# Cosine attention and an MLP mixer in one kernel: norms pair by pair, another order of squares, loads and sums, two more pairs transposed on TensorE

## The chip, the cores and the metric

The kernel runs on one NeuronCore of a Trainium2 chip. The metric is the device time of one execution in microseconds (us). Before the change it was 390.23 us, the median of three runs (390.15 to 393.83).

## The reference

For each of 8 batches and 12 heads, q, k and v are 448 x 64 matrices. Cosine attention divides each row of q and k by its norm, multiplies, divides by tau = 0.1, takes the softmax and multiplies by v. The heads side by side give x, 448 x 768 for each batch. The mixer then works along the tokens and along the channels:

```
q_n = q / (norm(q) + 1e-6);  k_n = k / (norm(k) + 1e-6)
attn = softmax(q_n @ k_n^T / tau);  x = attn @ v           (heads side by side)
h = relu(x^T @ w_tok1) @ w_tok2;   u = x + h^T             (w_tok1 448x256, w_tok2 256x448)
out = u + relu(u @ w_ch1) @ w_ch2                          (w_ch1 768x1536, w_ch2 1536x768)
```

The kernel leaves out the subtraction of the row's maximum (a cosine divided by tau is at most 10) and gets the sum of the exponentials from a column of ones beside v.

## The kernel before

Heads are worked in pairs, six pairs to a batch, 48 pairs in all. A pair is 128 columns of x. The kernel calls `manual_schedule`, so the order of the source is the order of each engine's queue; a wait therefore holds everything behind it on that engine. The instructions of SP are DMA issues, in the same order.

What is done for one pair i:

- `load_qk`, `load_v` (L122, L134): DMAs issued on SP. From pair 12 on the last 64 rows of k and v are fetched for three pairs at a time (`load_rest`).
- `squares` (L242): POOL multiplies q and k by themselves, into one of three `sq` buffers. In the first turns ACT does a part.
- `sums` (L260): VectorE adds each row's squares, into `ssq`.
- `norms` (L266): in one form ACT takes Ln and Exp (scale 0.5), which is the norm, into `ne` beside a constant 1e-6, and VectorE adds the two (L273) and takes the reciprocal (L274). In the other form (`act=True`) ACT does four steps, Ln, Exp, Ln with 1e-6 added, Exp. Pairs 0 to 17 (`SINGLE`) use the first form, each by itself; the others use the second, three pairs at a time.
- `scaled` (L303): POOL multiplies q and k by the reciprocal norms and writes fp16 (`kq16`).
- `tpose` (L307) turns q and k with eight TensorE transposes and one VectorE copy (L318); `tpose_dma` (L320) does it with one DMA transpose on SP. Pairs from `DMA_T0` = 13 on use the DMA.
- `score` (L332) and `score_rest` (L343): matmuls, and ACT's exponentials into `pt`.
- `pv_rest`, `pv` (L351, L364): pt times v into two PSUM tiles psO, one for each head; VectorE takes the reciprocal of the sums (L381) and multiplies (L382), which gives x. For the first pairs `pv_wide` (L386) does both heads in one tile.
- `tok1` (L403): x times w_tok1 into psR, VectorE's relu into `rt` (L412). `tok2` (L414): rt times w_tok2 into psU, and VectorE's add gives u (L426). u is then turned by a DMA transpose (`udma`, L430) or on TensorE (`upose`, L434) into `ut`.

When all pairs of a batch are through, its channel mixing is put in a queue of units (`refill`, L519): 12 units `m_ch1` (L442: six matmuls into psG, ACT's relu) and 6 or 8 units `m_ch2` (L457: twelve matmuls into psF, VectorE's add of u into `ost`, L469, and the store). A budget (`fed`) decides how many units follow in each turn: `unit(True)` always, and further ones while the budget lasts.

PSUM has two pools. `ps2`, tag "s", has three buffers of two banks: scores, psQ, `pv_wide`'s psO, and each turn's units called with True. `ps`, tag "b", has two buffers of one bank: the transposes' results, psR, psU, the two psO tiles, and further units.

From pair 7 on, the turn of pair i has this order (L670 to L704): three scores of pair i; `pv_rest` and `pv` of pair i-1; `side(i)`, which holds loads, squares, cast of v, sums, norms, scaling and the DMA transpose for pairs further on; a unit; the rest of the scores; `tok2(i-2)`; a TensorE transpose of pair i+1, if it has one; further units; `tok1(i-1)`; and, up to turn 15, `sums`. `SQ_AT` and `SU_AT` (L524, L525) say which pairs' squares and sums come in turns 12 to 15, where the lead of the squares grows from three pairs to five. Loads run six pairs ahead up to turn 14, and seven from there.

Of the kernel before, what the change touches and what calls it, by code (L numbers as in the profile page):

```python
# [7 lines left out]
FP32 = mybir.dt.float32  # L8
# [14 lines left out]
def kernel(  # L23
# [12 lines left out]
    nc = tc.nc  # L36
# [16 lines left out]
    EPS_NORM = 1e-6  # L53
    DMA_T0 = 13
    OLD = 2 * NPAIR
    SINGLE = 3 * NPAIR

# [87 lines left out]
    nc.gpsimd.memset(tiny[:], 1e-18)  # L145
    eps = cst.tile([128, 1], FP32, name="eps")
    nc.gpsimd.memset(eps[:], EPS_NORM)

# [100 lines left out]


    def sums_of(i):
        n, col, w = (-1 - i, 0, 1) if i < SINGLE else (i // HP, i % HP, HP)
        h = half.setdefault(n, {})
        if "ssq" not in h:
            tag = "" if w > 1 else "1"
            h["ssq"] = nrm.tile([128, w, 2 * QS], FP32, name=f"ssq_{i}", tag="ssq" + tag, bufs=4)
            h["rn"] = nrm.tile([128, w, 2 * QS], FP32, name=f"rn_{i}", tag="rn" + tag, bufs=4)
        return h, col

    def sums(i, a0=0, a1=2):  # L260
        n, sl = some(i, a0, a1)
        h, col = sums_of(i)
        nc.vector.tensor_reduce(out=h["ssq"][0:n, col, sl], in_=pipe[i]["sq"][0:n, sl],  # L263
                                axis=AXX.X, op=ALU.add)

    def norms(i0, i1, a0=0, a1=2, dve=False, act=False):  # L266
        h, col = sums_of(i0)
        n, sl = some(i0, a0, a1)
        ssq = h["ssq"][0:n, col:col + i1 - i0, sl]
        rn = h["rn"][0:n, col:col + i1 - i0, sl]  # L270
        ne = nes[i0 % 3][0:n, sl]
        if dve:
            nc.vector.tensor_reduce(out=rn[:, 0], in_=ne, axis=AXX.X, op=ALU.add)  # L273
            nc.vector.reciprocal(out=rn, in_=rn)  # L274
            return
        nc.scalar.activation(out=rn, in_=ssq, func=AF.Ln, bias=tiny[0:n])
        nc.scalar.activation(out=rn if act else ne[:, :, 0], in_=rn if act else rn[:, 0], func=AF.Exp, scale=0.5)
        if act:
            nc.scalar.activation(out=rn, in_=rn, func=AF.Ln, bias=eps[0:n])
            nc.scalar.activation(out=rn, in_=rn, func=AF.Exp, scale=-1.0)  # L280

    def scale(i, a, eng=None):
        st = pipe[i]
        eng = eng or nc.gpsimd
        sl, np_ = lay(i)
        if "kq16" not in st:
            st["kq16"] = kqs[i % 4]
        kq, p = st["kq16"], np_[a]
        h, col = sums_of(i)
        rn = h["rn"][:, col, sl[a]]  # L290
        n = KC if a == 0 and not old(i) else NCH
        eng.tensor_tensor(out=kq[0:p, a, 0:n].rearrange("p c g e -> p g c e"),  # L292
                          in0=st["kq"[a]][:].rearrange("p (g c) e -> p g c e", g=2),
                          in1=_bcast_free(rn[0:p, 0:2 * n].rearrange("p (g c) -> p g c", g=2), E), op=ALU.mult)
        if n == KC:
            if i < OLD + 4:
                eng.memset(kq[:, 0, KC].rearrange("p g e -> p (g e)"), 0.0)
            for g in range(2):
                p = slice(64 * g, 64 * g + 64)
                eng.tensor_scalar(out=kq[p, 0, KC, g], in0=half[i // HP]["kr"][p, i % HP],  # L300
                                  scalar1=rn[p, 2 * KC:KS], scalar2=1.0, op0=ALU.mult, op1=ALU.mult)
# [84 lines left out]
    def pv_wide(i):  # L386
# [5 lines left out]
        for hh in range(2):  # L392
            for m, lo in enumerate(windows(i // NPAIR)):
                for c in range(NCH):
                    at = (2 * c + hh) * S + lo
                    nc.tensor.matmul(o[:, hh, m, 0:E + 1], pts[i % 2][0:SC, at:at + 128],
                                     vt[0:SC, i % HP, NCH * hh + c, 0:E + 1], start=(c == 0), stop=(c == NCH - 1))
        rec = att.tile([128, 2, 4], FP32, name=f"rec_{i}", tag="rec2", bufs=2)
        nc.vector.reciprocal(out=rec[:], in_=o[:, :, :, E])
# [14 lines left out]
    def tok2(i, pe=False, wide=False):  # L414
        st = pipe[i]
        b, pj = i // NPAIR, i % NPAIR
        if pj == 0:
            u16[b] = mix.tile([128, DT, 4, 128], FP16, name=f"u16_{b}", tag="u16", bufs=4)
            ut[b] = mix.tile([128, DT, 4, 128], FP16, name=f"ut_{b}", tag="ut")
        psU = (ps2 if wide else ps).tile([128, 4, 128], FP32, name=f"psU_{i}", tag="s" if wide else "b")  # L420
# [9 lines left out]
    def udma(i):  # L430
        b, pj = i // NPAIR, i % NPAIR
        nc.sync.dma_start_transpose(out=ut[b][:, pj], in_=u16[b][:, pj].rearrange("p m d -> p (m d)"))

    def upose(i, n=1):  # L434
        b, pj = i // NPAIR, i % NPAIR
        psT = ps.tile([128, n, 4, 128], FP16, name=f"psT_{i}", tag="b")
        for j in range(n):
            for m in range(4):
                nc.tensor.transpose(psT[:, j, m], u16[b][:, pj + j, m], id16[:])
        nc.vector.tensor_copy(out=ut[b][:, pj:pj + n], in_=psT[:])  # L440

    def m_ch1(b, ct, wide):  # L442
# [5 lines left out]
        for dt in range(DT):  # L448
            nc.tensor.matmul(psG[:, 0:S], wc1t[:, dt, ct * 128:(ct + 1) * 128],  # L449
                             ut[b][:, dt].rearrange("p m s -> p (m s)")[:, lo:lo + S],  # L450
                             start=(dt == 0), stop=(dt == DT - 1))
# [71 lines left out]

    SQ_AT = {12: [15, 16], 13: [17], 14: [18, 19], 15: [20]}  # L524
    SU_AT = {15: [18, 19]}  # L525

    with tc.manual_schedule():
# [16 lines left out]
        sums(0, 1, 2)  # L544
        norms(0, 1, 1, 2)
        sums(0, 0, 1)
        norms(0, 1, 1, 2, dve=True)
        norms(0, 1, 0, 1)
        scale(0, 1, nc.vector)
        norms(0, 1, 0, 1, dve=True)  # L550
        scale(0, 0)
# [4 lines left out]
        sums(1)  # L556
        norms(1, 2)
        tpose(0, 1, 2)
# [6 lines left out]
        score(0, 1)  # L565
        norms(1, 2, dve=True)
        scale(1, 0)
        scale(1, 1, nc.vector)
        sums(2)
        norms(2, 3)  # L570
        cast_v(0)
# [4 lines left out]
        warm(6)  # L576
        norms(2, 3, dve=True)
        square(3, 1, act=True)
# [4 lines left out]
        for i in range(1, NPAIR):  # L583
# [10 lines left out]
            sums(i + 2)  # L594
            norms(i + 2, i + 3)
            if i >= 2:
                tok1(i - 2)
            pv_wide(i - 1)
            norms(i + 2, i + 3, dve=True)
            cast_v(i)  # L600
# [20 lines left out]
        sums(i + 2)  # L621
        norms(i + 2, i + 3)
        tok1(i - 2)
        pv_wide(i - 1)
        norms(i + 2, i + 3, dve=True)
        cast_v(i)
# [7 lines left out]
        tok1(i - 1)  # L634
        tok2(i - 2, pe=True)

        def side(i):
            single = i + 2 < SINGLE  # L640
            t = i + (6 if i <= 14 else 7)
            if t < NP_ALL and i + 2 < DMA_T0:
                load_qk(t)
            sq = [n for n in SQ_AT.get(i, [i + 3 if single else i + 5]) if n < NP_ALL]
            for n in sq[0:1]:
                squares(n)
            cast_v(i)
            if i in (8, 10):
                weights_ch2((i - 8) // 2)
            if single:  # L650
                norms(i + 2, i + 3)
                norms(i + 2, i + 3, dve=True)
            elif i + 4 < NP_ALL:
                sums(i + 4)
                if (i + 4) % HP == 2:
                    norms(i + 2, i + 5, act=True)
            if i + 2 < NP_ALL:
                scaled(i + 2)
                if i + 2 >= DMA_T0:
                    tpose_dma(i + 2)  # L660
            for n in sq[1:]:
                squares(n)
            if t < NP_ALL and i + 2 >= DMA_T0:
                load_qk(t)
            if i + 4 < NP_ALL:
                load_v(i + 4)
            if i == 14:
                load_qk(i + 7)

        for i in range(NPAIR + 1, NP_ALL):  # L670
            b, pj = i // NPAIR, i % NPAIR
            for c in range(KC):
                score(i, c)
            if i == NPAIR + 1:
                tok2(i - 2, pe=True)
                upose(i - 4, 2)
                upose(i - 2)
                sums(i + 2)
            pv_rest(i - 1)
            pv(i - 1, 0)  # L680
            pv(i - 1, 1)
            if i == NPAIR + 1:
                refill(0)
            elif pj == 2 and b > 1:
                refill(b - 1)
            side(i)
            fed[0] += fed[1]
# [5 lines left out]
            if i > NPAIR + 1:  # L693
                tok2(i - 2)
            if i + 1 < DMA_T0:
                tpose(i + 1)
            if due():
                unit(True)
            while due():
                unit()  # L700
            tok1(i - 1)
            if i + 2 < SINGLE:
                for t in SU_AT.get(i, [i + 3]):
                    sums(t)  # L704
        last = NP_ALL - 1
# [49 lines left out]
```

## Time and profile before

| | |
|---|---|
| median of three runs | 390.23 us |
| the profiled execution | 391.75 us |
| its span, first to last instruction | 390.0 us |
| granted TensorE clock, mean | 0.993 of full speed |
| TensorE busy | 372.2 us, 95% |
| VectorE busy | 209.0 us, 54% |
| ACT busy | 224.6 us, 58% |
| POOL busy | 237.3 us, 61% |

The profile is one execution on the chip. A group of instructions is named by line, engine and operation, with its tiles as output<-input; PE is TensorE's matmuls, PEld its weight loads, DVE VectorE. A timeline's row has the start and the duration in us, and in brackets how long the engine was idle before it and who ended that. The ends of matmuls are modelled and overlap, so the distance from one start to the next is the better measure of TensorE's work.

### The profile page before, as it was taken

The page shows a single profiled execution, that of the slowest core. Times are in us where ns is not written, and L with a number is a line of the kernel's source. Part 1 is how long each engine was busy: PE and PEld are TensorE (multiplying, and loading weights), DVE is VectorE, ACT ScalarE, POOL GpSimd, SP SyncE. Part 2 cuts the span into 40 slices and gives each one's busy share as a digit, 9 for nine tenths or more (in the row PEclk, how much of TensorE's full clock was granted, in tenths as well). Part 3 has the DMA queues.
Part 4 walks back from the last instruction along what each step waited for, and adds up shares of the span by engine and source line. Part 5 has one row for each costly group of instructions (what it writes and reads, how often), then busy time and mean ns, then how long its engine had stood idle before and what let it go on. Part 6 is the DMA issues. An engine that isn't in the chain of part 4 may idle for free.

```text
span 390.0 us, 10129 instructions
## 1 busy us (share of the span) xinstructions
PE 372.2 (95%) x4100; PEld 241.4 (62%) x4100; DVE 209.0 (54%) x457; ACT 224.6 (58%) x378; POOL 237.3 (61%) x384
## 2 busy tenths in 40 slices
PE   5888999988899999999999999999999999999995
PEld 5566666666556666666556666667656666565563
DVE  7799766775635673556534574456534553241031
ACT  5999687755575537755575547754574546501500
POOL 8899979796787674948577684848685540000000
PEclk9899999999999999999999999999999999999999
DMA  8999999989797988867897799876997392023023
GB/s 231 281 223 216 183 252 220 186 197 209 188 217 169 195 187 200 190 145 145 172 207 176 180 211 202 181 157 149 177 235 134 75 178 69 13 55 96 0 76 88
DMA packets 117055, 65.00 MB, mean 167 GB/s; under 512 B 74896, under 2 KB 113424, under 8 KB 117008
## 3 DMA queue, kind: packets, MB, share of 16 engines
q1 hardware_dynamic: 112112, 58.41, 69.5%
q0 software_dynamic: 4080, 5.21, 7.8%
q10 hardware_dynamic: 816, 0.73, 0.6%
q8 instruction: 32, 0.52, 0.6%
q14 instruction: 15, 0.12, 0.1%
HBM read 43.45 MB, written 11.01 MB: 140 GB/s over the span
## 4 chain that ended last, share of the span: by engine, by line
PE 79%; ACT 7%; DMA 5%; DVE 3%; POOL 3%; issue 1%; SPq 1%; POOLq 0%; ACTq 0%; DVEq 0%
PE psG L449 27%; PE psF L465 25%; PE psO L378 9%; PE psS L339 6%; ACT pt L340 5%; PE psU L423 5%; PE psR L409 4%; POOL sq L240 2%; DMA kf<-in_k_dram 2%; PE psQ L346 2%; DMA ut<-u 2%; PE psO L361 1%; DMA qk<-kq 1%; ACT sq L238 1%; DVE ost L469 1%
## 5 line engine op out<-in xcount | busy, mean ns | idle before, releaser
L340 ACT ACTIVATE pt<-psS 128x896 f16<-128x896 f32 (+1 forms) x156 | 132.5, 916 | 54.4 <-PE psS L339 54.4
L449 PE MATMUL psG<-ut,wc1t 128*128 128x448 f16 x576 | 116.8, 352 | 0.5 <-DMA ut<-u 0.3
L465 PE MATMUL psF<-wc2t,gt 128*128 128x384 f16 (+2 forms) x684 | 116.2, 323 | 0.0
L465 PEld LDWEIGHTS <-gt 128*128 128x128 f16 x684 | 64.2, 98 | 38.0
L452 ACT ACTIVATE gt<-psG 128x448 f16<-128x448 f32 x96 | 51.4, 542 | 59.9 <-PE psG L449 59.9
L449 PEld LDWEIGHTS <-wc1t 128*128 128x128 f16 x576 | 53.9, 98 | 45.0 <-DVE u L426 0.6
L292 POOL TENSOR_TENSOR kq<-kf,rn 128x384 f16<-128x384 f32 (+1 forms) x48 | 42.8, 892 | 50.2 <-ACT rn L280 45.1
L469 DVE TENSOR_TENSOR ost<-psF,u 128x384 f32<-128x384 f32 (+2 forms) x65 | 35.6, 548 | 62.9 <-PE psF L465 61.5
L263 DVE TENSOR_REDUCE ssq<-sq 128x15 f32<-128x960 f32 (+2 forms) x49 | 55.7, 1140 | 3.9 <-ACT sq L238 3.8
L412 DVE TENSOR_SCALAR rt<-psR 128x256 f16<-128x256 f32 x48 | 20.1, 419 | 62.0 <-PE psR L409 61.9
L240 POOL TENSOR_TENSOR sq<-kf 128x384 f32<-128x384 f32 (+1 forms) x46 | 40.1, 872 | 18.8 <-DMA kf<-in_k_dram 18.6
L292 POOL TENSOR_TENSOR kq<-qf,rn 112x512 f16<-112x512 f32 x45 | 46.9, 1043 | 3.0
L339 PE MATMUL psS<-qk 64*128 64x448 f16 x312 | 42.1, 358 | 6.1 <-DVE qk L318 2.4
L240 POOL TENSOR_TENSOR sq<-qf 112x512 f32<-112x512 f32 x39 | 40.5, 1039 | 0.0
L378 PE MATMUL psO<-vt,pt 128*128 128x65 f16 (+1 forms) x1056 | 40.3, 193 | 0.2 <-DVE ut L440 0.2
L378 PEld LDWEIGHTS <-pt 128*128 128x128 f16 (+1 forms) x1056 | 35.2, 97 | 4.0 <-PE psS L339 1.0
L382 DVE TENSOR_TENSOR x<-psO,rec 128x256 f16<-128x256 f32 x84 | 35.6, 424 | 2.9
L426 DVE TENSOR_TENSOR u<-psU,x 128x512 f16<-128x512 f32 x48 | 33.0, 687 | 5.1 <-PE psU L423 3.6
L381 DVE RECIPROCAL rec<-psO 128x4 f32<-128x4 f32 x84 | 14.8, 176 | 30.6 <-PE psO L378 30.5
L409 PEld LDWEIGHTS <-w1t 128*128 128x128 f16 x384 | 24.9, 98 | 8.6 <-issue 1.9
L423 PEld LDWEIGHTS <-w2t 128*128 128x128 f16 x384 | 24.9, 98 | 7.8 <-issue 1.5
L423 PE MATMUL psU<-rt,w2t 128*128 128x128 f16 x384 | 29.3, 219 | 0.2 <-DVE qk L318 0.2
(58 smaller groups left out, 274.4 us busy)
## 6 DMA issues: line engine op xcount, KB each, us to landing
qf<-in_q_dram SPq DMA_DIRECT2D x48, 224.0 KB, 3.6
kf<-in_k_dram SPq DMA_DIRECT2D x36, 192.0 KB, 3.3
vf<-in_v_dram SPq DMA_DIRECT2D x36, 192.0 KB, 3.5
vf<-in_v_dram SPq DMA_DIRECT2D x12, 224.0 KB, 7.3
out_dram<-ost SPq DMA_DIRECT2D x8, 336.0 KB, 3.7
wc1t<-in_moe_w_ch_dram POOLq DMA_DIRECT2D x4, 576.0 KB, 9.8
wc2t<-in_moe_w_ch_dram POOLq DMA_DIRECT2D x2, 1152.0 KB, 12.7
out_dram<-ost SPq DMA_DIRECT2D x8, 288.0 KB, 3.1
```

Of the source, the lines that this page charges most:

```text
L240: nc.gpsimd.tensor_mul(out=dst, in0=src, in1=src)
L263: nc.vector.tensor_reduce(out=h["ssq"][0:n, col, sl], in_=pipe[i]["sq"][0:n, sl], axis=AXX.X, op=ALU.add)
L292: eng.tensor_tensor(out=kq[0:p, a, 0:n].rearrange("p c g e -> p g c e"), in0=st["kq"[a]][:].rearrange("p (g c) e -> p g c e", g=2), in1=_b ...
L339: nc.tensor.matmul(psS[:, hh, 0:S], qk[hb, c * n:c * n + 128], qm[hb], start=True, stop=True)
L340: nc.scalar.activation(out=pts[i % 2][0:n, 2 * S * c:2 * S * (c + 1)].rearrange("p (h s) -> p h s", h=2), in_=psS[0:n, :, 0:S], func=AF.Ex ...
L378: nc.tensor.matmul(psO[:, m, 0:E + 1], pts[i % 2][0:n, at:at + 128], vt[0:n, i % HP, nch * hh + c, 0:E + 1], start=(old(i) and c == 0), st ...
L409: nc.tensor.matmul(psR[:, tt], w1t[:, w1[m], tt * 128:(tt + 1) * 128], st["x"][:, m], start=(m == 0), stop=(m == 3))
L423: nc.tensor.matmul(psU[:, m], w2t[:, tt, lo:lo + 128], st["rt"][:, tt], start=(tt == 0), stop=(tt == TT - 1))
L449: nc.tensor.matmul(psG[:, 0:S], wc1t[:, dt, ct * 128:(ct + 1) * 128], ut[b][:, dt].rearrange("p m s -> p (m s)")[:, lo:lo + S], start=(dt ...
L452: nc.scalar.activation(out=gt[:, ct, (b % 2) * S:(b % 2 + 1) * S], in_=psG[:, 0:S], func=AF.Relu)
L465: nc.tensor.matmul(psF[:, 0:hi - lo], gt[:, ct, at:at + 128], wc2t[:, ct, lo:hi], start=(ct == 0), stop=(ct == CT - 1))
L469: nc.vector.tensor_tensor(out=o[p0:p1, lo:hi].rearrange("p (j e) -> p j e", e=128), in0=psF[p0:p1, 0:hi - lo].rearrange("p (j e) -> p j e" ...
```

## The change

- `norms` has one form only: each pair by itself, ACT's Ln and Exp, VectorE's add and reciprocal, for all 48 pairs. `SINGLE`, the tiles for three pairs, and the four ACT steps are gone.
- `side` is split in `squared` (loads, squares, cast of v) and `turned` (norms, scaling, DMA transpose, later loads). Squares are three pairs ahead, loads six, in all turns.
- `sums(i + 3)` comes in every turn directly ahead of `tok1(i - 1)`.
- `DMA_T0` is 15: pairs 13 and 14 are turned on TensorE.
- `ut` is a tile for each pair and not one for the batch; the buffers take the same space. `upose` does one pair at a time.
- `pv_wide` is cut in two: the reciprocal and the product are `x_wide`.
- Turn 7 has another order: `tok2` of pair 4 moves there from turn 6, pair 6 goes through `pv_wide`, and `turned` comes after the fourth score.

```
-    DMA_T0 = 13
+    DMA_T0 = 15
...
     def sums_of(i):
-        n, col, w = (-1 - i, 0, 1) if i < SINGLE else (i // HP, i % HP, HP)
...
+        st = pipe[i]
+        if "ssq" not in st:
+            for nm in ("ssq", "rn"):
+                st[nm] = nrm.tile([128, 1, 2 * QS], FP32, name=f"{nm}_{i}", tag=nm, bufs=4)
+        return st
...
-    def norms(i0, i1, a0=0, a1=2, dve=False, act=False):
+    def norms(i, a0=0, a1=2, dve=False):
...
         nc.scalar.activation(out=rn, in_=ssq, func=AF.Ln, bias=tiny[0:n])
-        nc.scalar.activation(out=rn if act else ne[:, :, 0], in_=rn if act else rn[:, 0], func=AF.Exp, scale=0.5)
-        if act:
-            nc.scalar.activation(out=rn, in_=rn, func=AF.Ln, bias=eps[0:n])
-            nc.scalar.activation(out=rn, in_=rn, func=AF.Exp, scale=-1.0)
+        nc.scalar.activation(out=ne[:, :, 0], in_=rn, func=AF.Exp, scale=0.5)
...
+        st["psO"] = o
+
+    def x_wide(i):
+        st = pipe[i]
+        o = st["psO"]
         rec = att.tile([128, 2, 4], FP32, name=f"rec_{i}", tag="rec2", bufs=2)
...
-            ut[b] = mix.tile([128, DT, 4, 128], FP16, name=f"ut_{b}", tag="ut")
+            ut[b] = [mix.tile([128, 4, 128], FP16, name=f"ut_{b}_{j}", tag=f"ut{j}") for j in range(DT)]
...
-    SQ_AT = {12: [15, 16], 13: [17], 14: [18, 19], 15: [20]}
-    SU_AT = {15: [18, 19]}
...
         tok1(i - 1)
-        tok2(i - 2, pe=True)
...
-        def side(i):
...
+        def squared(i):
+            if i + 2 < DMA_T0:
+                load_qk(i + 6)
+            if i + 3 < NP_ALL:
+                squares(i + 3)
             cast_v(i)
             if i in (8, 10):
                 weights_ch2((i - 8) // 2)
...
+        def turned(i):
             if i + 2 < NP_ALL:
+                norms(i + 2)
+                norms(i + 2, dve=True)
                 scaled(i + 2)
                 if i + 2 >= DMA_T0:
                     tpose_dma(i + 2)
+                    if i + 6 < NP_ALL:
+                        load_qk(i + 6)
             if i + 4 < NP_ALL:
                 load_v(i + 4)
...
             if i == NPAIR + 1:
+                tok2(i - 3, pe=True)
                 tok2(i - 2, pe=True)
-                upose(i - 4, 2)
+                upose(i - 4)
+                pv_wide(i - 1)
+                upose(i - 3)
                 upose(i - 2)
+                x_wide(i - 1)
                 sums(i + 2)
...
+                squared(i)
+            else:
+                pv_rest(i - 1)
+                pv(i - 1, 0)
+                pv(i - 1, 1)
+                if pj == 2 and b > 1:
+                    refill(b - 1)
+                squared(i)
+                turned(i)
             fed[0] += fed[1]
             unit(True)
...
             if i > NPAIR + 1:
                 tok2(i - 2)
+            else:
+                turned(i)
             if i + 1 < DMA_T0:
                 tpose(i + 1)
             if due():
                 unit(True)
             while due():
                 unit()
+            if i + 3 < NP_ALL:
+                sums(i + 3)
             tok1(i - 1)
-            if i + 2 < SINGLE:
-                for t in SU_AT.get(i, [i + 3]):
-                    sums(t)
```

## The prediction

> **What bounds it now.** I read the busy rows first, then the waits, then the order of work on TensorE and VectorE. The page gives each engine's busy time:
>
> ```profile
> PE 372.2 (95%) x4100; PEld 241.4 (62%) x4100; DVE 209.0 (54%) x457; ACT 224.6 (58%) x378; POOL 237.3 (61%) x384
> ```
>
> In the table of stretches of 8 us TensorE is busy for all 8.00 us in nearly every stretch from 104 us to 384 us, and the chain that ended last is 79% PE. So from 104 us on an edit is worth what it adds to TensorE's queue or how long it keeps that queue waiting. Before 40 us the chain runs through ACT's exponentials, and between 76 and 103 us through POOL and DMA. The list of waits shows what stands still (who waited <- for whom: us in total, times, longest):
>
> ```profile
> DVE rt L412 <- PE psR L409: 61.9, 23, 4.3
> ...
> PE psS L339 <- DMA qk<-kq: 2.4, 3, 1.1
> ...
> PE psO L361 <- POOL vt L220: 1.1, 1, 1.1
> ...
> PE psG L449 <- DMA ut<-u: 0.3, 1, 0.3
> ```
>
> The last three rows are all of TensorE's waits after 76 us that this change could remove. The first tells the opposite: VectorE usually sits waiting for psR, so psR is evacuated (rt) the moment it is ready. That is what the change touches.
>
> A "turn" of pair i starts with its first score matmul. Turn 26 starts at 175.70. The end of turn 25 on VectorE, and the same stretch on TensorE (start us, us, ...):
>
> ```profile
> 175.36 0.56 DVE L469 TENSOR_TENSOR ost<-psF,u 128x384 f32<-128x384 f32 x1 [1.26 <-PE psF L465]
> 175.83 0.41 DVE L412 TENSOR_SCALAR rt<-psR 128x256 f16<-128x256 f32 x1
> 177.09 0.18 DVE L381 RECIPROCAL rec<-psO 128x4 f32<-128x4 f32 x1 [0.85 <-PE psO L378]
> ```
>
> ```profile
> 175.15 0.61 PE L409 MATMUL psR<-x,w1t 128*128 128x128 f16 x8
> 175.70 0.74 PE L339 MATMUL psS<-qk 64*128 64x448 f16 x6
> 176.28 0.30 PE L361 MATMUL psO<-vt,pt 64*128 64x65 f16 x8
> ```
>
> rt ends at 175.83 + 0.41 = 176.24, and psO's first matmul starts at 176.28. The psR, psU, psT and psO tiles share the two buffers of tag "b" in pool `ps`; pv_rest (L361) alternates between two psO tiles, so it needs both, and psR's must be free. There are 0.04 us of slack.
>
> Does a late rt hold TensorE, one for one? The profile has a case. Turn 20 ends with a unit of two adds:
>
> ```profile
> 139.56 1.12 DVE L469 TENSOR_TENSOR ost<-psF,u 64x384 f32<-64x384 f32 x2 [1.26 <-PE psF L465]
> 140.71 0.42 DVE L412 TENSOR_SCALAR rt<-psR 128x256 f16<-128x256 f32 x1
> ```
>
> ```profile
> 139.90 0.55 PE L339 MATMUL psS<-qk 64*128 64x448 f16 x4
> 140.74 0.36 PE L339 MATMUL psS<-qk 64*128 64x448 f16 x2 [0.29 <-DVE ost L469]
> 140.94 0.53 PE L361 MATMUL psO<-vt,pt 64*128 64x65 f16 x8
> 141.40 0.93 PE L378 MATMUL psO<-vt,pt 128*128 128x65 f16 x24
> 142.16 2.11 PE L465 MATMUL psF<-wc2t,gt 128*128 128x384 f16 x12
> ```
>
> From psR's start to rt's end it takes 141.13 - 139.35 = 1.78 us here, against 176.24 - 175.15 = 1.09 in turn 25: 0.69 later. From the turn's first score to the unit behind psO TensorE takes 142.16 - 139.90 = 2.26 us, against 177.27 - 175.70 = 1.57: 0.69 more. One for one (part of it through the score tile that waits for the add).
>
> **Part 1, the place of sums: the term that decides.** After the change sums(i+3) stands between the turn's units and tok1(i-1), so on VectorE the queue is: last unit's ost, ssq, rt. Before, it stood behind rt (turns to 15) or in the middle of the turn (from 16). Its row:
>
> ```profile
> L263 DVE TENSOR_REDUCE ssq<-sq 128x15 f32<-128x960 f32 (+2 forms) x49 | 55.7, 1140 | 3.9 <-ACT sq L238 3.8
> ```
>
> The 128x960 form is 1.14 us; the next instruction starts 1.06 us after it (164.59 and 165.65 in turn 24). In a turn whose last unit is a psF one, ost ends too late for ssq to go anywhere but in front of rt: rt starts 1.06 us later, ends at 177.30 in the example, and psO waits until 177.35 rather than 176.30: 1.05 us. In a turn that ends with psG units ACT empties them, VectorE has been free since u, and ssq is long done: nothing. TensorE's timeline gives the turns with sums whose last unit before psR is psF: 12, 14, 18, 19, 20, 24, 25, 26, 30, 31, 32, 36, 37, 38, 42, 43, 44. That is 17 x 1.05 = **+17.9**. Bounds: 0.9 each (a little of ssq under slack in some turns) to 1.2 (all of 1.14 and a hand-over), 15.3 to 20.4.
>
> The Trainium skill, "Perfetto Trace Analysis", Optimizing Tensor Performance, asks that independent matmul groups rotate through PSUM banks so that an evacuation overlaps the next group. By that rule the late rt would be overlapped and the term zero; the case at 139.56 says that two buffers are used up here, and the measurement decides.
>
> **Part 2, pairs 13 and 14 on TensorE, loads and squares.** It removes the two earliest of 35 DMA transposes of kq, and the ramp of squares from three to five pairs ahead in turns 12 to 15, for which POOL waited on kf (3.65 us longest, at 100.06) with the load's issue behind a transpose on SP. Squares three ahead of loads six ahead have three turns for the load. So four late starts go: scores of turns 13, 14, 15 begin 0.34, 1.19, 1.05 us after the place where psR's 0.54 would let them, psO after turn 16's scores 1.22 late (102.92 against 101.12 + 0.58): **-3.8** (by starts; the waits' rows give less, since they count from modelled ends). For: pair 15's transpose is issued when POOL has scaled it, near 86.4, lands 3.3 (median) to 5.9 (longest) us later, by 92.3, needed near 94. Bounds: -3.8 to -1.7 (if 15's and 16's stay).
>
> Added: 2 x 8 transposes; eight cost 0.44 us of TensorE's queue (psR's eight of the same shape at 78.62 to the next group): **+0.9**. Turn 13 has one unit and no other cover: behind it VectorE does u (0.69), the qk copy (0.68), ssq and rt, psR waits for u's buffer and the scores for the copy. Laying these rows end to end from psU's end I get 6.5 us from psO to psO where 5.1 would do: **+1.4** (0.5 to 2.0).
> The Trainium skill, "VectorE: DVE Perf Modes", Rules for kernel authors, prefers TensorE for a 128x128 transpose; its table has 390 ns for one. Sixteen would be 6.2 us by the page, as an estimate, and 0.9 by the rows; this case's TensorE is the bound, so the preference is no gain by itself.
>
> **Part 3, turn 7.** tok2(4) leaves turn 6, so turn 7's scores start after the qk copy (39.16, was 39.70), and the unit starts near 42.9 instead of 43.41. But norms(9), which now wait for copies, x_wide's x (0.69) and sums (1.2), stand ahead of the qk copy of pair 8 on VectorE: x 44.4, ssq 45.5, Ln and Exp 46.2, reduce and reciprocal 46.7, copy 47.3, scores of turn 8 at 47.35 (were 47.02), psO's second half behind ssq and rt another 0.2: **+0.6** (-0.5, the head start alone, to +1.5).
>
> **Part 4, norms by pair.** For 30 pairs ACT does 30 x (0.318 + 0.218) = 16.1 us instead of 10 x (0.33 + 0.24 + 0.33 + 0.24) = 11.4, VectorE 30 x (0.18 + 0.25) = 12.9 more. ACT waits 59.9 us for psG alone, VectorE 61.9 for psR; this is hidden: 0. The reduce waits for ACT behind x; ost and u are queued behind it, about 0.4 us later at most, and psF and psU have buffers to spare until the turn's end. POOL's scaling now always starts about 4 us into the turn and ends at 6.7, the DMA transpose lands about 11, is needed at 13.2 or later. Before, every third turn was like that (175.66 + 1.04, 7.6 us into turn 25, needed at 182.34) and held. SP issues about 6.2 us of work in a turn of 7.3, u's transpose behind the pair's. If SP slips, scores wait: 0 to +6, I take 0.
>
> **Part 5, ut per pair.** psG of a batch already starts five of its six matmuls (186.50) and waits only for the last one's transpose, 0.3 us. In turn 25 the pair's transpose now goes about 1 us earlier, and u's behind it 1 to 2: **-0.3** (0 to -0.3).
>
> **Sum:** 17.9 - 3.8 + 0.9 + 1.4 + 0.6 - 0.3 = +16.7. The profiled execution took 391.75 us (span 390.0), so 408.4 like for like; it lies 1.5 above the median of 390.23, so I forecast 390.23 + 16.7 = **406.9**.
>
> **Rivals.** (a) Sums cost nothing, because ssq is served in VectorE's idle time: -1.2 in all, 389.0, and with turn 7 at its better end 388. It is the first part alone that decides: under 1.2/17 = 0.07 us a turn the change is no loss. For it: VectorE is 54% busy. Against it: the idle time before the last ost is in front of an instruction that is ahead in the queue. (b) Half of it is hidden, 0.5 us a turn, since psO's first tile or the scores give slack: 17 x 0.5 - 1.2, 397.5. Against it: 0.04 us of slack. (c) SP's queue becomes a second wait: scores wait for qk (or psG for ut) in most turns, up to 6 more, 413. For it: SP works almost without a pause from 176.73 to 199; against it: the third turns of before. (d) The order does not end up as the source has it: then as (a).
>
> **Chances.** Forecast 0.74 (402 to 411), (a) with (d) 0.06, (b) 0.08, (c) 0.12. Range 400 to 412, from the bounds of part 1 (-2.6, +2.5) and the smaller ones, into (c). A measurement tells 1% here: faster 0.04, same 0.04, slower 0.92.
>
> **What would show it.** A new row of TensorE's waits, psO L361 on VectorE's rt, 15 to 18 times about 1 us, in the turns named, and none in those ending in psG; ssq directly before rt; no wait of POOL's squares for kf; no psS wait for qk near 79 to 101. The forecast is wrong if psO starts within 0.6 us of the scores in turn 26, or if waits for qk stand beside it.

## The result, and the profile after

The changed kernel takes 413.42 us, the median of four runs (410.33 to 413.97), against 390.28 us; the ratio is 1.0554, with a 95% interval of 1.0474 to 1.0633. It is slower by 5.5%, as forecast in sign. The median is 1.4 us above the upper end of the stated range (400 to 412) and 6.5 above the forecast of 406.9; by the ratio it is 390.23 x 1.0554 = 411.9 us, just inside the range.

The span went from 390.0 to 411.9 us. TensorE's waits after the change (who waited <- for whom: us in total, times, longest us):

```profile
PE psO L349 <- DVE rt L405: 16.8, 18, 1.2
...
PE psG L441 <- DMA ut<-u: 1.6, 1, 1.6
PE psF L457 <- DMA wc2t<-in_moe_w_ch_dram: 1.3, 1, 1.3
```

The first row did not exist before: 18 times TensorE stands in front of psO for the evacuation of psR, about 0.93 us each. The rows for the DMA of qk (2.4 us) and for vt (1.1) of the kernel before are gone. Two rows for DMAs are new, or larger than before.

One of the 18 places, the end of turn 25, on VectorE and on TensorE (start us, us, engine, line, operation):

```profile
184.63 0.56 DVE L461 TENSOR_TENSOR ost<-psF,u 128x384 f32<-128x384 f32 x1 [1.26 <-PE psF L457]
185.11 1.14 DVE L256 TENSOR_REDUCE ssq<-sq 128x15 f32<-128x960 f32 x1
186.17 0.41 DVE L405 TENSOR_SCALAR rt<-psR 128x256 f16<-128x256 f32 x1
```

```profile
184.43 0.61 PE L402 MATMUL psR<-x,w1t 128*128 128x128 f16 x8
184.98 0.74 PE L327 MATMUL psS<-qk 64*128 64x448 f16 x6
185.55 0.19 PE L349 MATMUL psO<-vt,pt 64*128 64x65 f16 x1
186.64 0.28 PE L349 MATMUL psO<-vt,pt 64*128 64x65 f16 x7 [0.89 <-DVE rt L405]
```

ssq sits between ost and rt, and rt ends at 186.58. psO's first tile gets its one matmul at 185.55, and the second tile waits until 186.64. TensorE's next unit starts 2.62 us after the turn's first score (187.60 - 184.98), against 1.57 before: 1.05 us lost.

The rest of the difference lies early and late. I call lag the start of a turn in a kernel less the start of the same turn in the kernel before, both from the profiles. The lag of the changed kernel is 0.77 us at turn 6, 0.24 at turn 7 (`tok2` of pair 4 no longer stands in front of it), 2.83 at turn 9, 4.91 at turn 17, 18.49 at turn 44 and 22.37 at turn 46.

In turn 45 there is one thing that no wait explains. TensorE's row after the longest of the waits, and the stretches of 8 us around it (busy time and instructions of TensorE, its weight loads, VectorE, ACT and POOL, then the granted clock, the DMA share and GB/s):

```profile
338.58 0.28 PE L349 MATMUL psO<-vt,pt 64*128 64x65 f16 x7 [1.25 <-DVE rt L405]
338.80 1.31 PE L366 MATMUL psO<-vt,pt 128*128 128x65 f16 x24
339.91 3.39 PE L457 MATMUL psF<-wc2t,gt 128*128 128x384 f16 x12
```

```profile
328.00:336.00 8.00, 7.11 (x88) 4.84 (x85) 4.90 (x12) 3.49 (x6) 3.23 (x6) 1.00 0.36 93
336.00:344.00 8.00, 6.46 (x65) 3.80 (x62) 4.64 (x12) 3.42 (x6) 2.58 (x5) 0.79 0.43 98
```

The twelve psF matmuls take 3.39 us where they take 2.11 elsewhere, at a granted clock of 0.79 in that stretch: 1.6 us with psO's, in one turn.

### The profile page after: what moved, and what is told of

It is laid out like the page before. It is cut to its first block, busy times and chain, and to the rows that moved or that the text cites. A ratio compares the mean times of both kernels' runs of the same rounds, so it can differ in the third digit from the quotient of the medians.

```text
span 411.9 us, 10191 instructions
## 1 busy us (share of the span) xinstructions
PE 377.5 (92%) x4116; PEld 243.6 (59%) x4116; DVE 221.8 (54%) x518; ACT 226.8 (55%) x398; POOL 237.8 (58%) x383
## 4 chain that ended last, share of the span: by engine, by line
PE 72%; DVE 11%; DMA 10%; ACT 3%; POOL 2%; issue 1%; ACTq 0%; POOLq 0%; DVEq 0%
PE psF L457 27%; PE psG L441 25%; PE psO L366 8%; DVE ssq L256 6%; PE psU L416 4%; DMA wc2t<-in_moe_w_ch_dram 3%; DMA ut<-u 3%; PE psS L327 3%; DVE ost L461 3%; PE psR L402 2%; DMA w2n<-in_moe_w_tok_dram 2%; PE psO L349 2%; PE psQ L334 2%; DVE rt L405 2%; ACT pt L328 1%
## 5 line engine op out<-in xcount | busy, mean ns | idle before, releaser
L457 PE MATMUL psF<-wc2t,gt 128*128 128x384 f16 (+2 forms) x684 | 117.7, 325 | 1.3 <-DMA wc2t<-in_moe_w_ch_dram 1.3
L280 POOL TENSOR_TENSOR kq<-kf,rn 128x384 f16<-128x384 f32 (+1 forms) x48 | 42.9, 894 | 98.0 <-DVE rn L266 91.9
L335 ACT ACTIVATE pt<-psQ 128x448 f16<-128x448 f32 x36 | 19.5, 541 | 36.1 <-PE psQ L334 36.1
L402 PE MATMUL psR<-x,w1t 128*128 128x128 f16 x384 | 29.3, 219 | 0.4 <-DVE u L419 0.3
```

The costliest lines, as they stand in the source:

```text
L402: nc.tensor.matmul(psR[:, tt], w1t[:, w1[m], tt * 128:(tt + 1) * 128], st["x"][:, m], start=(m == 0), stop=(m == 3))
L457: nc.tensor.matmul(psF[:, 0:hi - lo], gt[:, ct, at:at + 128], wc2t[:, ct, lo:hi], start=(ct == 0), stop=(ct == CT - 1))
```

## The experiments

They ran on three chips, each beside the kernel before, whose median differed: 392.46 us for the first three experiments and for turns 6 and 7 in the order of before, 391.2 us for the last one, 390.69 us for the other four. So the ratios count more than the medians. Times in the heads of the paragraphs are medians.

**Sums behind rt.** The two lines that part 1 blames are moved, and nothing else.

```
-            if i + 3 < NP_ALL:
-                sums(i + 3)
             tok1(i - 1)
+            if i + 3 < NP_ALL:
+                sums(i + 3)
```

> Sums put behind tok1 in every turn, all else as in the changed kernel. Theory (the place of ssq ahead of rt costs 1.06 us in each of 17 turns that end with a psF unit, 1.18 in two of them): the waits of psO for rt go, and the time falls by about 18, from 413.4 to about 395. Rival (the order of queues elsewhere, SP or POOL by now, holds the turns): psO's waits go and others take their place, the time stays over 405.

Measured: 390.61 us, ratio to the kernel before 0.9973 (0.9933 to 1.0012). In turn 25 of this kernel VectorE and TensorE now read:

```profile
175.86 0.56 DVE L461 TENSOR_TENSOR ost<-psF,u 128x384 f32<-128x384 f32 x1 [1.26 <-PE psF L457]
176.33 0.41 DVE L405 TENSOR_SCALAR rt<-psR 128x256 f16<-128x256 f32 x1
176.66 1.14 DVE L256 TENSOR_REDUCE ssq<-sq 128x15 f32<-128x960 f32 x1
```

```profile
176.20 0.74 PE L327 MATMUL psS<-qk 64*128 64x448 f16 x6
176.78 0.30 PE L349 MATMUL psO<-vt,pt 64*128 64x65 f16 x8
```

No wait of psO for rt is left. Moving two lines gives back the whole loss, 4 us more than I expected: the wait of 0.8 us behind turn 13 went with the others, the early loss was smaller in this run (lag of 1.40 at turn 9), and the granted clock stays at 1.00 from 16 us to the last matmul. In this profile the other parts of the change add up to nothing: the lag at turn 47 is 0.05 us.

**Sums ahead of the turn's further units.** Again only the place, now in VectorE's idle time while psF is computed.

```
             if i + 1 < DMA_T0:
                 tpose(i + 1)
+            if i + 3 < NP_ALL:
+                sums(i + 3)
             if due():
                 unit(True)
             while due():
                 unit()
-            if i + 3 < NP_ALL:
-                sums(i + 3)
             tok1(i - 1)
```

> Sums put behind tok2 and ahead of the turn's further units, so that they run while psF is computed. Theory (VectorE's idle time before the last ost takes them whole): as with sums behind tok1, about 395, and turn 13, which has no further unit, keeps its wait. Rival (it is the amount of VectorE's work in a turn, not its place): little gain, over 405.

Measured: 392.37 us, ratio 1.0013 (0.9975 to 1.0051). The same amount of work on VectorE, in another place:

```profile
175.20 1.14 DVE L256 TENSOR_REDUCE ssq<-sq 128x15 f32<-128x960 f32 x1
176.54 0.56 DVE L461 TENSOR_TENSOR ost<-psF,u 128x384 f32<-128x384 f32 x1 [0.20 <-PE psF L457]
177.01 0.41 DVE L405 TENSOR_SCALAR rt<-psR 128x256 f16<-128x256 f32 x1
```

ssq ends at 176.34, and ost still waits 0.20 us for psF. So it was never the amount. Turn 13, which has no further unit, keeps its wait of 0.6 us for rt, as expected.

**The same cost in the kernel before.** A reduction of the same shape, without use, ahead of tok1.

```
+            if 12 <= i < NP_ALL - 3:
+                nc.vector.tensor_reduce(out=extra[:], in_=zz, axis=AXX.X, op=ALU.add)
             tok1(i - 1)
```

> The kernel before, with one more reduction of 128x960 fp32 (its result is not used) ahead of tok1 in turns 12 to 44, and nothing else. Theory (one for one): 15 turns from 18 on at 1.06 are 15.9, turns 12 and 14 partly under the waits for qk that they have anyway, so 390.3 + 16 to 17.5 = 406 to 408. Rival (VectorE at 54% has room for 1.1 us a turn): 390 to 393.

Measured: 409.46 us, ratio 1.0507 (1.0410 to 1.0604); its profiled run took 408.63. TensorE's new wait is the one of the changed kernel to within 0.1 us:

```profile
PE psO L365 <- DVE rt L416: 16.9, 18, 1.2
```

From turn 18 on the lag grows by 1.06 us in each turn that ends with a psF unit (1.18 where that unit has two adds, and 0.61 in turn 26, whose delay swallows the wait for ut that the kernel before has next), and in no other. It is 1.15 at turn 18 and 16.99 at turn 47, inside what was expected; the median is 1.5 us above it. This one instruction put in front of rt makes the kernel before as slow as the changed one but for some 4 us.

**rt on ACT.** The changed kernel with its sums where they are; psR of pairs 11 and on is emptied by another engine.

```
+        if i >= 11:
+            nc.scalar.activation(out=st["rt"][:], in_=psR[:], func=AF.Relu)
+            return
         nc.vector.tensor_scalar_max(out=st["rt"][:], in0=psR[:], scalar1=0.0)
```

> The changed kernel with its sums ahead of tok1 as they are, but rt of pairs 11 and on taken by ACT in place of VectorE. Theory (psO waits for the buffer of psR, which is emptied late only because rt queues behind ssq on VectorE): the waits of psO for rt go, 413.4 - 18 = 395 or somewhat less. Rival (psO is late because of ssq itself, or because of what POOL and ACT deliver to the next turn): over 405.

Measured: 390.76 us, ratio 0.9969 (0.9935 to 1.0004). On VectorE ssq still follows ost; on ACT:

```profile
177.07 0.38 ACT L406 ACTIVATE rt<-psR 128x256 f16<-128x256 f32 x1 [2.30 <-PE psR L402]
177.37 2.54 ACT L328 ACTIVATE pt<-psS 128x896 f16<-128x896 f32 x3
```

ACT had been idle for 2.30 us. psO starts 0.57 us after the scores, and its waits for rt are gone. So ssq itself holds nobody; what held TensorE was psR, full behind it.

**Turns 6 and 7 in the order of before.**

```
         tok1(i - 1)
+        tok2(i - 2, pe=True)
...
             if i == NPAIR + 1:
-                tok2(i - 3, pe=True)
                 tok2(i - 2, pe=True)
                 upose(i - 4)
-                pv_wide(i - 1)
                 upose(i - 3)
                 upose(i - 2)
-                x_wide(i - 1)
                 sums(i + 2)
+                pv(i - 1, 0)
+                pv(i - 1, 1)
                 refill(0)
                 squared(i)
+                turned(i)
...
-            else:
-                turned(i)
```

> Turns 6 and 7 in the order of the kernel before (tok2 of pair 4 in turn 6, pv and not pv_wide, norms ahead of the unit), all else as in the changed kernel. Theory (the 2.3 us lost in turn 7 come from its order, and the wait of psF for wc2t of 1.3 in turn 12 follows from it, since that load is issued 2.8 later): 413.4 - 2.3 - 1.4 = 409.7, no wait for ut in turn 7 and none for wc2t. Rival (both waits are slower transfers in this run, whatever the order): within 1 us of 413.4, waits still there.

Measured: 410.6 us, ratio 1.0510 (1.0445 to 1.0574), between the two expectations and nearer the first. The lag grows by 0.31 us from turn 6 to turn 9, against 2.06 in the changed kernel, and psG's wait for ut is gone. (The 2.3 us of the expectation are counted from turn 7; 0.5 of them are `tok2` of pair 4, which the change only moves from turn 6 to turn 7.) The wait for wc2t fell to 0.6 us, but see below: it is not the order of turn 7 that makes it. This profile too has a stretch at a granted clock of 0.79 (240 to 248 us), in turn 33.

**DMA for pairs 13 and 14, with sums behind rt** (`DMA_T0 = 13`).

> Sums behind tok1 as in the first experiment, and pairs 13 and 14 turned by DMA again (DMA_T0 = 13). Theory (with loads six and squares three ahead in all turns, the two DMA transposes land in time, so turning the pairs on TensorE only adds its 0.9 and the wait for u and the copy in turn 13): 1.4 to 1.9 less than with sums behind tok1 alone (390.6), about 389. Rival (the DMA transposes themselves were what made turns 13 to 15 late): scores wait for qk again, 1 to 2 more, 392.

Measured: 391.37 us, ratio 1.0003 (0.9968 to 1.0037): no gain that can be told. The profile says why. From turn 12 to turn 17 this kernel catches up 2.43 us on the kernel before, against 0.90 with the TensorE transposes, so the theory's 1.5 us are there, and no score waits for qk; but from turn 6 to turn 9 it lost 1.81, with a wait of 1.6 us for ut, where the version with sums behind rt alone lost 0.79.

**Turns 6 and 7 as before, with sums behind rt.**

> Sums behind tok1, and turns 6 and 7 in the order of before. Theory (the order of turn 7 costs 1.3 there, and half of the wait for wc2t follows from it): 390.6 - 1.3 - 0.6 = 388.7. Rival (turn 7 only moves a wait that comes later anyhow): 390 to 391.

Measured: 390.79 us, ratio 0.9982 (0.9955 to 1.0008). The time can't be told from that without this edit, and the profiles say why. From turn 6 to turn 9 this version loses 0.67 us and the one without the edit 0.79; the 1.3 us of the expectation were counted from turn 7, and 0.5 of them are the moved `tok2`. So next to that run there was hardly anything to gain. Over all profiles turns 6 to 8 lose 0.8 to 2.1 us in the order of the change (five profiles) and 0.3 to 0.7 in the order of before (four). psF's wait for wc2t is 0.9 us here and 1.2 in the next version, which has this order too: it does not follow from turn 7.

**All three.**

> Both of these at once: sums behind tok1, turns 6 and 7 as before, pairs 13 and 14 turned by DMA. Theory (the three costs add): 390.6 - 1.9 - 1.6 = 387.1, under both kernels. Rival (one of the two brings back a wait for qk or for ut): 389 or more.

Measured: 389.93 us, ratio 0.9967 (0.9941 to 0.9994); the profiled span is 387.9. It has the lowest median of the study, 0.3% under the kernel before (rt on ACT has a ratio as low, 0.9969), and is 2.8 us slower than my sum. The lag is -1.97 us at turn 47, 2.0 below that with sums behind rt alone, where my sum had 3.5; a wait of 1.2 us for wc2t is still in it.

**And wc2t's second half a turn earlier** (in turns 8 and 9 in place of 8 and 10).

> As the version with sums behind tok1, turns 6 and 7 as before and pairs 13 and 14 turned by DMA, and the second half of wc2t loaded in turn 9 and not in turn 10. Theory (wc2t lands 13.9 us after its issue and the first psF unit waits 1.2 us for it): the wait goes, 389.9 - 1.2 = 388.7. Rival (the load only moves into other transfers, k, v and u land later and something else waits): 389.5 to 390.5.

Measured: 390.29 us, ratio 0.9982 (0.9955 to 1.0009). The wait for wc2t is gone, and this has come:

```profile
PE psS L327 <- DMA qk<-kq: 3.4, 3, 1.5
```

The rival held: the scores of pairs 13, 14 and 15 now wait for their DMA transposes. The first was issued at 75.51 us and took 5.6 us, where the version without this edit has 74.26 and 4.0. How the load of wc2t delays it was not tested by itself.

## Why the prediction was right, and where its sizes were off

The sum forecast +16.7 us; the lag in the profile is 22.4. Every sign that was to show it came: 18 waits of psO for rt, 17 of them behind the turns named, none behind a turn that ends with psG units, ssq directly ahead of rt, no wait of POOL's squares for kf and none of the scores for a DMA of qk.

**Part 1, the place of sums: right, and settled.** Forecast 17 x 1.05 = 17.9; the changed kernel's turns show 14 x 1.06 + 3 x 1.18 = 18.4, in the 17 turns named and in none of those that end with psG units. Undone, moved to idle time, added to the kernel before, or with rt on another engine, it behaves as a wait for psR's buffer. The case at 139.56 that it leaned on was mixed, since 0.29 of its 0.69 us were the scores' wait for ost; the added reduction is the clean one. Rival (a), that VectorE's idle time takes it, needed an order that the queue did not have; the second experiment gave it that order, and there it holds. Rival (b), half hidden, fell: the 0.04 us of slack were all there was. Rival (c), SP's queue, fell too: no score waited for a DMA of qk after the change, and psG waited for ut once. Rival (d), another order than the source's, fell with the rows of VectorE.

**Part 2: right in its sizes, but the gain has another cause.** The late starts of turns 13 to 15 and of psO in turn 16 shrank by 0.33, 1.13, 1.05 and 1.22 us, 3.7 (forecast 3.8). Added were 0.44 in turn 12, 1.02 in turn 13 and 0.80 in front of the next psO, 2.3 (forecast 0.9 + 1.4). But turning pairs 13 and 14 on TensorE was not what removed the waits: with the new loads and squares the DMA transposes land in time (unless wc2t's load comes a turn earlier, as the last experiment has it), and from turn 12 to turn 17 the profiles with `DMA_T0` = 13 (and wc2t's load where it was) gain 1.5 and 1.0 us on the same versions without it. The times do not show it clearly.

**Part 3, turn 7: the sign right, the wait that made the size left out.** +0.6 was forecast, 2.1 measured (the lag goes from 0.77 at turn 6 to 2.83 at turn 9). I reckoned the unit's start (42.9) from TensorE and VectorE alone. It started at 43.71, did two of six matmuls and waited for u of pair 2 until 45.81:

```profile
43.71 0.54 PE L441 MATMUL psG<-ut,wc1t 128*128 128x448 f16 x2
45.81 0.92 PE L441 MATMUL psG<-ut,wc1t 128*128 128x448 f16 x4 [1.56 <-DMA ut<-u]
```

That transpose was issued at 32.72 and landed 13.0 us later, beside weights and loads. In the kernel before it was issued at 31.36, took 11.9 us and landed at 43.24, 0.2 ahead of psG's start:

```profile
43.41 1.30 PE L449 MATMUL psG<-ut,wc1t 128*128 128x448 f16 x6
```

The unit ran into a transfer that had no more slack, and norms, the qk copy and turn 8's scores queued behind it. How late it lands goes with the run: in the five profiles with this order the lag at turn 9 is 1.4 to 1.6 us where it landed by 44.6, and 2.5 to 2.8 where it landed at 45.4 or later. I had not looked at this transfer; the median of 3.6 us for its kind would have been the wrong row.

**Parts 4 and 5: right.** POOL waits 91.9 us for norms instead of 45.1, and TensorE's waits for POOL did not grow (1.0 us for kq, 0.9 before, and none for vt). The wait for ut cost 0.46 less in turn 27 (forecast 0.3), with sums behind rt too; a tile for each pair was not tested by itself.

**What the sum left out:** the wait for wc2t in turn 12 (+1.5 by starts), the drop of the clock in turn 45 (+1.6), and 0.8 in the first turns, where the other profiles have 0.1 to 0.9, the kernel before with the extra reduction 0.4. With these 18.4 - 3.7 + 2.3 + 2.1 - 0.5 + 1.5 + 1.6 + 0.8 = 22.5, against a lag of 22.37 at turn 46. Parts 1 and 2 came to 17.0 where 16.4 was forecast; most of the other 5.4 us is from things that the sum did not have. The range reached to 412 for the sake of rival (c), which fell, so that it nearly covers the measured time is luck.

wc2t's second half landed 13.3 to 14.0 us after its issue in the changed kernel and in the seven versions of it that load it in turn 10, and 11.8 and 11.5 in the kernel before and in the one with the extra reduction. In the last two the next load of q is issued some 3 us behind it or later, in the others within 2 us of it. That these loads slow it would fit, and was not tested by itself.

## What to carry to other kernels

An evacuation of PSUM that the bound engine waits for must have nothing in front of it on its own engine that is still running when it could start, however idle that engine is on average. Here, with all buffers of the pool in use, a reduction put there was paid one for one in each turn in which VectorE was busy until then. Before moving an instruction into "idle time", look which instruction the idle time stands in front of: it helps only those queued ahead of that one. And where a change starts something earlier, look up the one transfer that it will meet (11.9 us here), not the median of its kind (3.6).

## What the runs showed of the hardware that I had not expected

The granted clock dropped for a short while in the middle of a run whose TensorE is busy 92%. In the changed kernel psF's weight loads from 340.22 to 342.46 start 0.32 us apart, about twice their usual distance, and then return to it. Between 16 us and the last matmul the profiles have two such drops, here and with turn 7 put back. Both come in the turn behind a psF unit with two adds, where TensorE stands longest, 1.25 us, and is busy for 1.5 us of 3. The same stretch stands at turns 21, 33 and 45 of these two profiles and of the kernel before with the extra reduction: nine times, with two drops. So it can bring a drop and need not.

The profiles show one thing that orders this. The clock was low from 339.09 to 342.50 us here and from 241.68 to 245.09 with turn 7 put back, 3.41 us each time, and the other changes of the clock in a profile lie whole multiples of 3.41 us from these (it falls next at 410.77, which is 20 of them on). Cut into such stretches, the one just ahead of each drop has TensorE busy for 55% by the profile's modelled ends. At full clock, all stretches of all profiles with 40% or less ended in a drop and none with 58% or more did; five others with 52 to 55% did not, so what decides there is open.

The Trainium skill, "TensorE: Matmul & The Clock Gate", What's actually happening, has the clock fall to half after an idle window of about 3.4 us. The length agrees with the 3.41 us here; but no idle stretch ahead of the two drops is near that long, so a stretch that was busy for about half of the time was enough. Its section on psum-queue depth-cycling tells of a clock that swings with short idle stretches between groups of matmuls; the two drops fit that better, and no run here was made to test it.
